# Two loads of the next batch moved ahead of the stores of the last one on SyncE's queue

## Chip, cores, metric

One core of one Trainium2 chip (trn2). The metric is the device time of one execution in microseconds (us), median over the runs. Only fast executions are compared.

## The reference, cut to what matters

Batched cross attention between x and a small state, followed by a feed-forward layer over all 4352 rows.

```python
B, H, S, Ns, D = (8, 8, 512, 32, 64)        # x: (B,H,S,D), state: (B,H,Ns,D)
scores = scale * x @ state^T                 # softmax -> xread = a  @ state
scores2 = scale * state @ x^T                # softmax -> sread = a2 @ x
t = concat([xread, sread], axis=2)           # -> rows of 512
h = t @ w_in                                 # 512 x 2048
g = h * sigmoid(1.702 * h)
out = g @ w_out                              # 2048 x 512
```

## The kernel before: the parts concerned

Batches 0 and 1 begin while the weights are still being converted to fp32. From batch 1 on, the product with w_out is done in Strassen's way (products called x, y, z below), and the attention of the next batch is cut into slots that are called after each half of a product. All loads and stores are issued on SyncE's queue, in program order (in before the last weight load at 121.77 us, the four stores from 157.78, the loads of batch 2 from 161.81).

```python
    def load_state(b):                       # 2 DMAs of 32 KB; two buffers
        stn[b] = apool.tile([P, NG, D], FP32, tag="stn", name=f"stn_{b}", bufs=2)
        for g in range(NG):
            nc.sync.dma_start(stn[b][:, g], st_v[b, g])

    def load_x(b):                           # 4 DMAs of 256 KB; one buffer (batch 1 has its own place)
        ...
        for c in range(SCH):
            nc.sync.dma_start(xn[b][:, c], x_v[b, c])

    def att_slots(b):                        # attention of batch b, slot by slot
        ...
        at(0, att_state, b)                  # transpose of the state
        for j in range(NPR):
            at(j, att_xT, b, j)              # four transposes of x each
        at(5, att_scores, b)
        ...

    def down(key, r, fs, dst, last):         # one row block f of w_out, for output rows r
        ...
        if fs[-1] == NF - 1:                 # after the last row block: store
            osb = opool.tile([P, DM], FP32, tag="osb", name=f"osb_{key}_{r}")   # two buffers
            nc.scalar.copy(osb, ops)
            nc.sync.dma_start(dst, osb)

        def product(ps, lhs, rhs, first):    # in strassen()
            for r in range(nb):              # nb = 2 halves of 16 matmuls at this size
                for f in range(HF):
                    nc.tensor.matmul(ps[:, r], lhs[f][:, P * r : P * (r + 1)], rhs[:, f], ...)
                if todo:
                    for fn, args in todo.pop(0):
                        fn(*args)

    for f in range(NF):                      # batch 0's product with w_out, 16 row blocks
        rounds(1)                            # VectorE converts weight pieces
        round_to(NFC * NPR + f + 1)
        for r in range(SCH):
            down(0, r, [f], out_x[0, r], r == SCH - 1)
        ...
        if f == NF - 2:
            T_of(T1, B12, B11)
            ...
    ...
    T_of(B12, B22, B12)
    T_of(T4, B21, T2)
    load_state(2)                            # behind the four stores of batch 0
    load_x(2)
```

Of the kernel before, what the change touches and what calls it, by code (L numbers as in the profile page):

```python
# [20 lines left out]
def kernel(  # L21
# [39 lines left out]
    NF = DF // P  # L61
# [58 lines left out]
    def load_state(b):  # L120
# [4 lines that stand above are left out]
    def load_x(b):  # L125
        if b == 1:
            xn[b] = sums[:, 0].rearrange("p (c h d) -> p c h d", c=SCH, h=H)
        else:
            xn[b] = xpool.tile([P, SCH, H, D], FP32, tag="xn", name=f"xn_{b}")
        for c in range(SCH):  # L130
            nc.sync.dma_start(xn[b][:, c], x_v[b, c])  # L131
# [89 lines left out]
    def round_to(n, ahead=AHEAD):  # L221

        while done["b"] < min(n, len(PIECES)):
            powers_to(min(done["b"] + 1 + ahead, max(NFC * NPR, done["b"] + 1)))
            round_b(done["b"])
            done["b"] += 1
            while done["b"] > NPR and done["load"] < len(PIECES) and before(done["load"]) < done["b"]:
                load_weights(done["load"] + 1)
# [114 lines left out]
    def att_M(b, c, spare=False):  # L343

        m = mpool.tile([P, NG, FC], FP32, tag="M", name=f"M_{b}_{c}")
        A[b]["M", c] = m
        name = f"M_{b}_{c}_"
        ps = [psH.tile([P, FC], FP32, tag="h", name=name + str(g)) if spare else att_ps([P, FC], name + str(g)) for g in range(NG)]
        by_state(b, ps, lambda rows, j: w_in[c][rows, j])
        for g in range(NG):  # L350
            nc.scalar.copy(m[:, g], ps[g])  # L351

    def att_eT(b, g):

        a = A[b]
        if g == 0:
            a["eT"] = apool.tile([P, NG, SCH, P], FP32, tag="eT", name=f"eT_{b}")
        ps = att_ps([P, SCH, P], f"eT_{b}_{g}")
        for c in range(SCH):
            nc.tensor.transpose(ps[:, c], a["e2"][g][0][:, P * c : P * (c + 1)], ident)  # L360
        nc.scalar.copy(a["eT"][:, g], ps)

    def att_sread(b):

        a = A[b]
        ps = att_ps([P, NG, D], f"sr_{b}")
# [3 lines that stand above are left out]
                    st = slice(Ns * j, Ns * (j + 1))  # L370
                    nc.tensor.matmul(  # L371
                        ps[st, g], a["eT"][:, g, c, st], xn[b][:, c, NG * j + g],
                        start=(c == 0), stop=(c == SCH - 1),
                    )
        sr = apool.tile([P, P], FP32, tag="sr", name=f"sr_{b}")
        nc.scalar.copy(sr, ps.rearrange("p g d -> p (g d)"))
        A[b]["sr"] = sr

    def att_srT(b):
        ps = att_ps([P, P], f"srT_{b}")  # L380
        nc.tensor.transpose(ps, A[b]["sr"], ident)
        nc.scalar.copy(srT[:, :, b, :], ps.rearrange("p (j n) -> p j n", j=NPR))
# [35 lines left out]
    def up(key, f, ntok, lhs, rhs, spare=False):  # L418
        hps = att_ps([P, ntok], f"h_{key}_{f}") if spare else psH.tile([P, ntok], FP32, tag="h", name=f"h_{key}_{f}")
        n = len(lhs)  # L420
        for i in range(n):
            nc.tensor.matmul(hps, lhs[i], rhs[i], start=(i == 0), stop=(i == n - 1))  # L422
        if f % 2 == 0:
            G[key, f // 2] = free.pop(0)
        nc.scalar.activation(out=G[key, f // 2][:, f % 2, :ntok], in_=hps, func=AF.Gelu_apprx_sigmoid)  # L425

    def up_x(b, f, spare=False):
        c, o = divmod(P * f, FC)
        m = A[b]["M", c]
        up(b, f, S, [m[:, g, o : o + P] for g in range(NG)], [A[b]["aT"][:, g] for g in range(NG)], spare)  # L430
# [10 lines left out]
    def down(key, r, fs, dst, last):  # L441

        if fs[0] == 0:
            O[key, r] = psO.tile([P, DM], FP32, tag="o", name=f"o_{key}_{r}")
        ops = O[key, r]
        for f in fs:
            nc.tensor.matmul(  # L447
                ops, G[key, f // 2][:, f % 2, P * r : P * (r + 1)], w_out[:, f], start=(f == 0), stop=(f == NF - 1)
            )
            if last and f < HF and f % 2:  # L450
                free.append(G.pop((key, f // 2)))
        if fs[-1] == NF - 1:
            osb = opool.tile([P, DM], FP32, tag="osb", name=f"osb_{key}_{r}")
            nc.scalar.copy(osb, ops)
            nc.sync.dma_start(dst, osb)
# [10 lines left out]
    def s12(key, u, ntok):  # L466

        half = ntok // 2
        (a11, a21), (_, a22) = quarters(key, u, ntok), quarters(key, HF // 2 + u, ntok)
        s1, s2 = S1[:, 2 * u : 2 * u + 2, :half], S2[:, 2 * u : 2 * u + 2, :half]  # L470
        nc.vector.tensor_tensor(out=s1, in0=a21, in1=a22, op=ALU.add)  # L471
        nc.vector.tensor_tensor(out=s2, in0=s1, in1=a11, op=ALU.subtract)
# [167 lines left out]
    def rounds(n):  # L640
        round_to(done["b"] + n)
# [75 lines left out]
    def T_of(t, x0, x1):  # L717
        nc.vector.tensor_tensor(out=t, in0=x0, in1=x1, op=ALU.subtract)
# [3 lines left out]
    for f in range(NF):  # L722
        rounds(1)
# [3 lines that stand above are left out]
        if f in (0, 2):  # L727
            for g in range(NG):
                att_eT(f // 2, g)
        if f in (0, nper * 2):  # L730
            att_M(1, 2 + f // (nper * 2))
        if f in (1, 3):
            att_sread(f // 2)
        if f in (2, 4):
            att_srT(f // 2 - 1)
        if f % 2 == 1:
            up_x(1, rest.pop(0))
        if f == NF - 2:
            T_of(T1, B12, B11)
            for u in range(NU - 1):  # L740
                s12(1, u, S)
            T_of(T2, B22, T1)
# [2 lines left out]
        s3(1, u, S)  # L745
    T_of(B12, B22, B12)
    T_of(T4, B21, T2)
    load_state(2)
    load_x(2)

    nb = P // Ns
    for b in range(1, B):
# [45 lines left out]
```

## Time and profile before

| | before |
|---|---|
| median of the first 3 runs | 764.88 us (763.66 to 765.04) |
| span of the profiled execution | 762.4 us |
| TensorE busy | 746.1 us, 98% |
| x's first half to y's first half, batch 1 (161.26 to 176.21 us) | 14.95 us |
| the same place, batch 2, less two groups of other matmuls there | 7.90 us |

TensorE is nearly always busy, so the question is where it is not, or where its clock is low. The lines are in the prediction: a stall for the loads of state and x between the halves of product x, and a clock of 0.50 from about 3 us into it. How to read them: a timeline line gives start, length, engine, source line, what, and in brackets how long the engine was idle before it and what ended that; a windows line gives each engine's busy us in a stretch, then the granted clock of TensorE (1.00 is full), the DMA engines' busy share and GB/s. "The chain" is a third view: it follows the work that ended last back from each step to what released it. It counts overlapping matmuls once, so the 16 that take 3.62 us on the timeline take 3.45 there.

### The profile page before, as it was taken

The page shows a single profiled execution, that of the slowest core. Times are in us where ns is not written, and L with a number is a line of the kernel's source. Part 1 is how long each engine was busy: PE and PEld are TensorE (multiplying, and loading weights), DVE is VectorE, ACT ScalarE, POOL GpSimd, SP SyncE. Part 2 cuts the span into 40 slices and gives each one's busy share as a digit, 9 for nine tenths or more (in the row PEclk, how much of TensorE's full clock was granted, in tenths as well). Part 3 has the DMA queues.
Part 4 walks back from the last instruction along what each step waited for, and adds up shares of the span by engine and source line. Part 5 has one row for each costly group of instructions (what it writes and reads, how often), then busy time and mean ns, then how long its engine had stood idle before and what let it go on. Part 6 is the DMA issues. An engine that isn't in the chain of part 4 may idle for free.

```text
span 762.4 us, 9847 instructions
## 1 busy us (share of the span) xinstructions
PE 746.1 (98%) x4169; PEld 565.3 (74%) x4171; DVE 414.0 (54%) x712; ACT 231.8 (30%) x411; POOL 0.8 (0%) x8
## 2 busy tenths in 40 slices
PE   8989999989999999999999999999999999999997
PEld 3433444448788878887788778887888778888886
DVE  5999799640746465463636274637355560215511
ACT  4676511021414231433134141424143312104200
POOL 0000000000000000000000000000000000000000
PEclk9999999999999999999999999999999999999999
DMA  9821242040013000300040002100030000000001
GB/s 234 324 65 52 87 157 83 0 114 1 15 42 60 1 15 28 73 1 1 28 88 0 1 28 58 30 1 15 28 73 1 15 29 15 0 21 8 0 15 41
DMA packets 48763, 35.22 MB, mean 46 GB/s; under 512 B 36432, under 2 KB 44112, under 8 KB 48720
## 3 DMA queue, kind: packets, MB, share of 16 engines
q1 hardware_dynamic: 48720, 34.61, 15.8%
q8 instruction: 32, 0.52, 0.3%
q14 instruction: 11, 0.09, 0.0%
HBM read 25.69 MB, written 8.91 MB: 45 GB/s over the span
## 4 chain that ended last, share of the span: by engine, by line
PE 94%; SPq 2%; DMA 1%; ACT 1%; issue 0%; DVE 0%; ACTq 0%
PE y L494 19%; PE z L494 13%; PE x L494 13%; PE upy L578 8%; PE h L422 7%; PE o L447 7%; PE upz L578 5%; PE upx L578 5%; PE M L276 4%; PE h_sr L422 4%; PE xT L258 2%; SPq L131 1%; PE y_sr L494 1%; PE sr L371 1%; PE s L276 1%; PE z_sr L494 1%
## 5 line engine op out<-in xcount | busy, mean ns | idle before, releaser
L494 PE MATMUL x<-w_out,g 128*128 128x256 f32 x448 | 102.4, 385 | 0.0
L494 PEld LDWEIGHTS x<-w_out,g 128*128 128x128 f32 x448 | 85.9, 194 | 12.0 <-issue 0.5
L587 DVE TENSOR_TENSOR g<-upy,g 128x512 f32<-128x512 f32 x72 | 48.1, 689 | 68.7 <-PE upy L578 68.7
L584 ACT ACTIVATE g<-g 128x512 f32<-128x512 f32 x72 | 44.8, 630 | 84.8 <-DVE g L587 84.8
L422 PE MATMUL h<-aT,M 128*128 128x512 f32 x128 | 59.6, 611 | 4.4 <-ACT M L351 4.4
L351 ACT COPY M<-M 128x512 f32<-128x512 f32 x64 | 33.2, 596 | 95.0 <-PE M L276 95.0
L422 PEld LDWEIGHTS h<-aT,M 128*128 128x128 f32 x128 | 24.1, 194 | 37.6 <-issue 24.9
L494 PE MATMUL z<-sums,later 128*128 128x256 f32 x224 | 51.1, 382 | 0.0
L494 PE MATMUL z<-w_out,g 128*128 128x256 f32 x224 | 50.8, 382 | 0.0
L494 PE MATMUL y<-sums,g 128*128 128x256 f32 x224 | 50.5, 379 | 0.0
L494 PE MATMUL y<-sums,later 128*128 128x256 f32 x224 | 50.5, 379 | 0.0
L494 PE MATMUL y<-w_out,g 128*128 128x256 f32 x224 | 50.1, 382 | 0.0
L494 PEld LDWEIGHTS z<-sums,later 128*128 128x128 f32 x224 | 42.1, 190 | 10.5 <-issue 5.0
L494 PEld LDWEIGHTS y<-w_out,g 128*128 128x128 f32 x224 | 42.1, 190 | 10.5 <-issue 5.0
L578 PE MATMUL upy<-ta,M 128*128 128x256 f32 x192 | 49.3, 379 | 0.0
L578 PE MATMUL upx<-aT,M 128*128 128x256 f32 x192 | 49.3, 379 | 0.0
L494 PEld LDWEIGHTS z<-w_out,g 128*128 128x128 f32 x224 | 41.6, 190 | 6.2
L494 PEld LDWEIGHTS y<-sums,g 128*128 128x128 f32 x224 | 41.6, 190 | 5.2
L494 PEld LDWEIGHTS y<-sums,later 128*128 128x128 f32 x224 | 41.6, 190 | 5.2
L471 DVE TENSOR_TENSOR later<-g,g 128x512 f32<-128x512 f32 (+1 forms) x32 | 20.8, 651 | 40.7 <-ACT g L425 40.7
L511 DVE TENSOR_TENSOR osb<-z,later 128x512 f32<-128x512 f32 x14 | 9.7, 692 | 60.5 <-PE z L494 60.5
L578 PEld LDWEIGHTS upx<-aT,M 128*128 128x128 f32 x192 | 36.5, 190 | 5.0
(130 smaller groups left out, 1023.6 us busy)
## 6 DMA issues: line engine op xcount, KB each, us to landing
later<-in_moe_w_out_dram SPq DMA_DIRECT2D x16, 512.0 KB
out_dram<-osb SPq DMA_DIRECT2D x32, 256.0 KB
xn<-in_x_dram SPq DMA_DIRECT2D x28, 256.0 KB
w_out<-in_moe_w_in_dram SPq DMA_DIRECT2D x12, 512.0 KB
later<-in_moe_w_in_dram SPq DMA_DIRECT2D x4, 512.0 KB
sums<-in_x_dram SPq DMA_DIRECT2D x4, 256.0 KB
stn<-in_state_dram SPq DMA_DIRECT2D x16, 32.0 KB
out_dram<-osb_sr SPq DMA_DIRECT2D x4, 128.0 KB
```

Of the source, the lines that this page charges most:

```text
L131: nc.sync.dma_start(xn[b][:, c], x_v[b, c])
L258: nc.tensor.transpose(ps[:, c], x_heads(b, c, j), ident)
L276: nc.tensor.matmul(ps[g][st], A[b]["stT"][rows, st], rhs(rows, j), start=True, stop=True)
L351: nc.scalar.copy(m[:, g], ps[g])
L422: nc.tensor.matmul(hps, lhs[i], rhs[i], start=(i == 0), stop=(i == n - 1))
L447: nc.tensor.matmul(ops, G[key, f // 2][:, f % 2, P * r : P * (r + 1)], w_out[:, f], start=(f == 0), stop=(f == NF - 1))
L471: nc.vector.tensor_tensor(out=s1, in0=a21, in1=a22, op=ALU.add)
L494: nc.tensor.matmul(ps[:, r], lhs[f][:, P * r : P * (r + 1)], rhs[:, f], start=(first and r == 0 and f == 0), stop=(f == HF - 1), skip_grou ...
L511: nc.vector.tensor_tensor(out=o, in0=ps, in1=with_, op=ALU.add)
L578: nc.tensor.matmul(ps[:, k], lhs[:, o : o + P], rhs, start=(first and k == 0), stop=True, skip_group_check=True)
L584: nc.scalar.activation(out=dst, in_=src, func=AF.Gelu_apprx_sigmoid)
L587: nc.vector.tensor_tensor(out=dst, in0=ps, in1=x, op=ALU.add)
```

## The change

The loads of batch 2 have free buffers long before they are issued (batch 0's x was last read at 94.3 to 95.4 us, the loads go out from 161.81); SyncE, in order, stands at the stores, for 35.7 us before the first. So the loads are put ahead of them.

```diff
@@ -735,6 +735,9 @@
             att_srT(f // 2 - 1)
         if f % 2 == 1:
             up_x(1, rest.pop(0))
+        if f == NF - 4:
+            load_state(2)
+            load_x(2)
         if f == NF - 2:
             T_of(T1, B12, B11)
             for u in range(NU - 1):
@@ -745,8 +748,6 @@
         s3(1, u, S)
     T_of(B12, B22, B12)
     T_of(T4, B21, T2)
-    load_state(2)
-    load_x(2)
```

## The prediction

> **What bounds the kernel now.** I read the page first: if TensorE is busy almost all the time, a change can gain only where TensorE stands still or runs slowly.
>
> ```profile
> PE 746.1 (98%) x4169; PEld 565.3 (74%) x4171; DVE 414.0 (54%) x712; ACT 231.8 (30%) x411; POOL 0.8 (0%) x8
> ```
>
> TensorE is the bound; the chain that ended last is 94% TensorE by its own line on the page. Between 200 and 760 us it is busy 558.3 of 560 us, so nothing is to be had there. What the change touches is the loads of `xn` and `stn`, so I asked for TensorE's own waits between 140 and 200 us. There are only two kinds, and both are on these loads (total us, times, longest):
>
> ```profile
> PE xT L258 <- DMA xn<-in_x_dram: 3.0, 4, 0.9
> PE stT L249 <- DMA stn<-in_state_dram: 0.5, 1, 0.5
> ```
>
> Over the whole execution the first of these groups is the same 3.0 us and 4 times: batches 3 to 7 never wait for x. So there is a single place. The timeline of TensorE there (start, length, what, idle before and its releaser):
>
> ```profile
> 161.26 3.62 PE L494 MATMUL x<-w_out,g 128*128 128x256 f32 x16
> 165.36 0.30 PE L249 MATMUL stT<-ident,stn 128*128 128x128 f32 x1 [0.48 <-DMA stn<-in_state_dram]
> 166.48 0.30 PE L258 MATMUL xT<-ident,xn 128*128 128x128 f32 x1 [0.82 <-DMA xn<-in_x_dram]
> ...
> 169.84 0.48 PE L258 MATMUL xT<-ident,xn 128*128 128x128 f32 x1 [0.54 <-DMA xn<-in_x_dram]
> 170.11 5.82 PE L494 MATMUL x<-w_out,g 128*128 128x256 f32 x16
> 175.77 0.60 PE L258 MATMUL xT<-ident,xn 128*128 128x128 f32 x4
> 176.21 3.62 PE L494 MATMUL y<-sums,later 128*128 128x256 f32 x16
> ```
>
> Batch 1's first Strassen product x is cut in two groups of 16 matmuls. Between them stand the five transposes that begin batch 2's attention (one of the state, four of x), and TensorE runs in program order, so each of the five holds the second group until its load lands. The second thing to see is the length of that second group: 5.82 us for the same 16 matmuls that took 3.62 just before. The windows say why (busy us of each engine, then granted clock, DMA share, GB/s):
>
> ```profile
> 164.00:167.00 3.00, 1.47 (x7) 0.69 (x5) 3.00 (x5) 0.27 (x1) 0.00 (x0) 1.00 1.10 223
> 167.00:168.00 1.00, 0.37 (x1) 0.14 (x1) 1.00 (x1) 0.00 (x0) 0.00 (x0) 0.87 1.35 223
> 168.00:174.00 6.00, 4.63 (x12) 3.53 (x13) 2.32 (x2) 0.59 (x1) 0.00 (x0) 0.50 0.19 33
> 174.00:175.00 1.00, 1.00 (x5) 0.86 (x4) 0.00 (x0) 0.00 (x0) 0.00 (x0) 0.71 0.09 16
> 175.00:176.00 1.00, 1.00 (x8) 0.85 (x7) 0.00 (x0) 0.00 (x0) 0.00 (x0) 1.00 0.00 0
> ```
>
> The granted clock falls to a half about 3 us into the stall, and stays there until about 174.6, some 4.5 us after the last load landed. So the stall is paid twice: as waiting, and as slow matmuls afterwards. For comparison, the same place one batch later, where the loads had long landed (its clock is 1.00 throughout):
>
> ```profile
> 248.20 3.62 PE L494 MATMUL x<-w_out,g 128*128 128x256 f32 x16
> ...
> 253.38 0.27 PE L249 MATMUL stT<-ident,stn 128*128 128x128 f32 x1
> 253.49 0.60 PE L258 MATMUL xT<-ident,xn 128*128 128x128 f32 x4
> 253.93 3.62 PE L494 MATMUL x<-w_out,g 128*128 128x256 f32 x16
> ...
> 257.82 3.62 PE L494 MATMUL y<-sums,later 128*128 128x256 f32 x16
> ```
>
> Last, why the loads come late: the timeline of SyncE's queue.
>
> ```profile
> 121.77 0.33 SPq L160 DMA_DIRECT2D later<-in_moe_w_out_dram  x1
> 157.78 3.94 SPq L455 DMA_DIRECT2D out_dram<-osb  x4
> 161.81 1.13 SPq L123 DMA_DIRECT2D stn<-in_state_dram  x2
> 163.05 2.89 SPq L131 DMA_DIRECT2D xn<-in_x_dram  x4
> ```
>
> SyncE issues the last weight load at 121.77 us and then stands for 35.7 us (the queue's longest wait for ACT's osb copies) before the first of batch 0's four stores. The loads of batch 2 are behind these stores in the program, so they begin at 161.81 although their buffers were free long before: the old x of batch 0 was last read by its sread at 94.3 to 95.4 us, the old state before that.
>
> [...] six loads with nothing of their own to wait for stood behind the stores for 40 us. [...] 1.00 to 0.50 some 3 us into the stall, 0.50 for about 6.9 us (0.13 x 2 + 6 + 0.58, from the mean clocks of the windows). [...]
>
> **The change, part by part.** It adds and removes no instruction on any engine: the instruction order shows the same rows on TensorE, VectorE, ScalarE and GpSimd, and on SyncE only the six loads moved ahead of the four stores, right after the last load of w_out. "Four row blocks sooner" is where the lines stand in the program; what counts is when SyncE gets there, and it is free at 122.10 us (121.77 + 0.33).
> - *Loads.* Issue from 122.1, 3.2 us for six (161.81 to 164.98 now), the last piece landing 4.8 us after its issue (165.03 to 169.80 in the chain). Expected landed: 122.1 + 3.2 + 4.8 = 130.1, say 132 behind the weight load. They are needed at 164.9: over 30 us to spare.
> - *Waiting removed.* In the chain the first group of x ends at 164.88 and the second starts at 170.32: 5.44 us. Five transposes without waiting cost, from batch 3, 0.11 + 0.44 = 0.55 us in the chain. Removed: 5.44 - 0.55 = 4.89 us.
> - *Slow matmuls removed.* The second group takes 5.62 us in the chain, a warm one 3.45: 2.17 us, if the clock no longer falls.
> - *Stores.* They are issued when ACT's copies are done, 157.78 and on, as now, since SyncE has been idle for some 30 us by then. No cost.
> - *Sum.* 4.89 + 2.17 = **7.06 us**. Check by the other batch: x to y is now 176.21 - 161.26 = 14.95; one batch later 257.82 - 248.20 = 9.62, less the 8 up-projection matmuls between (two groups of 0.86 in the chain) 7.90. The difference is 7.05.
>
> All of it is on the path that sets the end: from 176 us on TensorE is busy without a gap worth naming, so what starts 7 us sooner ends 7 us sooner. From the median 764.88 that gives 757.8, from the profiled execution (764.29) 757.2. I predict **757.5 us**, 1.0% less.
>
> **The rivals.**
> 1. *Another wait takes the place of the one removed.* The y product would now start at about 169.3 instead of 176.2. It needs S2 and T2. VectorE's last S2 piece ends at 163.50 (162.81 + 0.69), T2 at 148.54: 5.8 us of slack are left. VectorE goes on with s3 and two T sums until 170.31, but their first user (y's second product, with T3 finished at 168.12) starts at 193.8 now and 186.7 then. VectorE's next task after them is 13.5 us idle ahead of it, ScalarE is idle 3 to 5 us before each x copy. The new order also shows y's matmuls waiting for two DMA semaphores that were not named there before; I read them as the old weight loads into the same buffer, or at worst batch 0's first stores, landed near 160.7 to 162. Each costs nothing. If instead y waited for the last T sum, 1 us would be lost: 758.5.
> 2. *Only the waiting goes, the clock falls all the same.* Then 4.9 us: 760. Against it: with the same work and no stall the clock is 1.00 in batches 3 to 7.
> 3. *The early loads collide.* They share the DMA engines with the last weight piece, and at 122 to 136 us VectorE is over 96% busy turning such pieces into w_out. But the last piece is first touched at 132.95, while it should land near 124.5, and TensorE is then some five row blocks behind VectorE (row block 12 is being converted at 122.4 and multiplied after 144). A few us of delay would be absorbed. If it were not: up to 1 or 2 us back, 759.
> 4. *Hidden anyway, gain near zero.* The waits named above speak against it.
>
> **Range and chances.** The gain is read off one profiled execution; the three times of before spread over 1.4 us, and the moment at which the clock comes back may vary by some tenths between executions. With rival 1's 1 us on one side and spread on both, I take 756.3 to 759.2. A gain of over 2% would need 749.6, twice what the stall is worth: 1%. Slower by over 2% would need a collision of 15 us: 0.5%. Within 2%: 98.5%.
>
> **What would show each step right or wrong.** In the profile after: the six loads at about 122 to 125.5 on SyncE's queue, the stores still near 157.8; no wait of TensorE for xn or stn after 100 us; five transposes taking about 0.6 us between the groups of x; the second group of x 3.62 us long, the clock 1.00 from 164 to 176; y starting near 169.2; everything from there to the end shifted by 7 us with equal durations. The prediction is wrong if y shows a wait of its own, if the clock still falls, if TensorE begins to wait for w_out between 122 and 160 us, or if a later batch waits for x or a store.

The sum is 4.89 + 2.17 = 7.06 us, both terms read from the trace. The 124.5 us of rival 3 is an estimate from the profile before, in which the DMA share is 0.65 from 124 to 124.5 us and 0.02 in the half microsecond after.

## The result, and the profile after

| | before | after |
|---|---|---|
| median | 764.65 us (763.66 to 765.04, 4 runs) | 757.47 us (757.20 to 757.98, 4 runs) |
| ratio of the fast runs | | 0.9909, 95% interval 0.9892 to 0.9926 |
| span of the profiled execution | 762.4 us | 755.7 us |
| mean granted clock | 0.993 | 0.998 |
| x's first half to y's first half | 14.95 us | 7.89 us |

A ratio is the mean time of one kernel's fast runs over that of the other's of the same rounds, so it is not quite the ratio of the medians. The interval lies clear of 1.

TensorE's timeline of the changed kernel at the same place:

```profile
161.62 3.62 PE L494 MATMUL x<-w_out,g 128*128 128x256 f32 x16
165.08 0.27 PE L249 MATMUL stT<-ident,stn 128*128 128x128 f32 x1
165.19 0.60 PE L258 MATMUL xT<-ident,xn 128*128 128x128 f32 x4
165.62 3.62 PE L494 MATMUL x<-w_out,g 128*128 128x256 f32 x16
...
169.51 3.62 PE L494 MATMUL y<-sums,later 128*128 128x256 f32 x16
```

No line has an idle time in brackets any more, and the second half of x takes 3.62 us where it took 5.82. The windows of the same kernel show the clock that goes with it:

```profile
167.00:168.00 1.00, 1.00 (x7) 0.87 (x5) 1.00 (x1) 0.00 (x0) 0.00 (x0) 1.00 0.00 0
168.00:174.00 6.00, 6.00 (x33) 5.31 (x32) 2.68 (x2) 1.47 (x3) 0.00 (x0) 1.00 0.01 3
```

And SyncE's queue of the changed kernel:

```profile
122.51 1.14 SPq L123 DMA_DIRECT2D stn<-in_state_dram  x2
123.69 3.67 SPq L131 DMA_DIRECT2D xn<-in_x_dram  x4
158.14 3.95 SPq L455 DMA_DIRECT2D out_dram<-osb  x4
```

The loads go out from 122.5 to 127.4 us and the DMA engines are idle again by about 130 (share 1.10 from 125 to 130 us, 0.03 from 130 to 135). The stores come out when ACT's copies are done, as before.

Where the 6.7 us of span went: the stage x to y is 7.06 us shorter (14.95 - 7.89), and the changed kernel's execution came to this stage 0.36 us later (161.62 against 161.26). Of that, 0.31 us is a group of 16 h matmuls at 42 us that took 8.83 us instead of 8.52, far ahead of the change; the experiment warm_start deals with that place.

### The profile page after: what moved, and what is told of

It is laid out like the page before. It is cut to its first block, busy times and chain, and to the rows that moved or that the text cites. A ratio compares the mean times of both kernels' runs of the same rounds, so it can differ in the third digit from the quotient of the medians.

```text
span 755.7 us, 9853 instructions
## 1 busy us (share of the span) xinstructions
PE 743.6 (98%) x4171; PEld 563.8 (75%) x4171; DVE 413.9 (55%) x712; ACT 231.7 (31%) x411; POOL 0.8 (0%) x8
## 4 chain that ended last, share of the span: by engine, by line
PE 96%; SPq 2%; ACT 1%; DMA 1%; issue 0%; DVE 0%; ACTq 0%
PE y L494 19%; PE z L494 13%; PE x L494 13%; PE upy L578 8%; PE h L422 8%; PE o L447 7%; PE upx L578 5%; PE upz L578 5%; PE M L276 4%; PE h_sr L422 4%; PE xT L258 2%; PE y_sr L494 1%; SPq L131 1%; PE sr L371 1%; PE s L276 1%; PE z_sr L494 1%
## 5 line engine op out<-in xcount | busy, mean ns | idle before, releaser
L494 PE MATMUL x<-w_out,g 128*128 128x256 f32 x448 | 100.2, 379 | 0.0
L494 PEld LDWEIGHTS x<-w_out,g 128*128 128x128 f32 x448 | 84.2, 190 | 11.4 <-ACT osb L454 0.2
```

## The experiments

Theory: the loads sat behind the stores for no reason of their own; TensorE paid for it twice, by 4.89 us of waiting and by 2.17 us of slow matmuls because its clock had fallen during the wait. (Of the 4.89 us, 3.52 are the idle times in brackets in the prediction's lines and others of the same kind; the other 1.37 are the five transposes, which take 1.92 us one by one and 0.55 in a row.) Rivals: the row block at which the loads stand matters; the DMA traffic itself costs something; the clock falls for another reason; the price is simply in proportion to the wait. Every kernel gave correct results. The runs below the first two rows of this table were done on three chips, each with its own runs of the kernel before (medians 764.53, 764.40 and 764.95 us). "x to y" is read from each kernel's own timeline, as above.

| run | x to y, us | median, us | ratio to before, 95% interval |
|---|---|---|---|
| (before) | 14.95 | 764.65 | |
| (after) | 7.89 | 757.47 | 0.9909 (0.9892 to 0.9926) |
| just_ahead | none: slow execution | 756.90 (the four fast) | 0.9905 (0.9890 to 0.9920) |
| just_ahead_2 | 7.89 | 756.90 | 0.9900 (0.9883 to 0.9917) |
| early_f3 | 7.90 | 757.63 | 0.9911 (0.9895 to 0.9927) |
| x_only | 8.55 | 757.95 | 0.9912 (0.9898 to 0.9927) |
| state_only | 13.34 | 761.97 | 0.9973 (0.9959 to 0.9988) |
| after_two | 9.83 | 759.29 | 0.9930 (0.9917 to 0.9943) |
| awake | 12.72 | 761.99 | 0.9974 (0.9957 to 0.9990) |
| slots_later | (other order) | 757.28 | 0.9906 (0.9891 to 0.9921) |
| warm_start | 7.90 | 755.85 | 0.9890 (0.9878 to 0.9903) |
| warm_before | 14.85 | 763.26 | 0.9978 (0.9964 to 0.9993) |

### Does the row block matter? just_ahead and early_f3

```diff
 # just_ahead: after row block 14, straight before the block that stores
-        if f == NF - 4:
+        if f == NF - 2:
             load_state(2)
             load_x(2)
 # early_f3: among the weight loads
-        if f == NF - 4:
+        if f == 3:
             load_state(2)
             load_x(2)
```

> The six loads stand after row block 14, just ahead of the four stores, instead of after row block 12. Theory (what counts is only to be ahead of the stores, since SyncE is free from 122 us): the queue issues them at the same 122 to 126 us, and the time is that of the changed kernel, 757.5 us (757.0 to 758.0). Rival (the row block at which they stand decides when they are issued): issue near 153 us; the time would still be about 757.5, but the queue's timeline would show it.

The first run's profile fell on an execution of 1313.42 us with a mean clock of 0.557, so nothing in it can be compared by time. Its other four took 755.83 to 757.86 us. The mean clock of that execution was 0.82 over the first 10 us, 0.55 from 10 to 100 us and 0.56 from 300 to 400 and from 1000 to 1300 us; nothing in these runs explains it. I repeated it:

> The kernel of just_ahead once more, unchanged: the profile of its first run fell on an execution at a clock of 0.56 throughout (1313 us), which cannot be laid beside the others. Expected in a fast execution: SyncE issues the six loads at 122 to 126 us, straight behind the last weight load, and the time is 757.5 us, or 755.9 us in executions whose clock shows 1.000.

The queue issued the state at 123.41 us, straight behind the last weight load (87.79 + 35.56 = 123.35), though the lines now stand behind row block 14. So "four row blocks sooner" is not what the change does: it takes the loads from behind the stores, which is 39 us sooner (161.81 - 122.51). The rival is out for places behind the last weight load. Ahead of it the place does move the issue, as the next run shows, but not the time.

> The six loads stand after row block 3, in the middle of the weight loads of w_out (ahead of the last six), where VectorE is busy without a gap and each weight load is issued only when a buffer comes free. Theory (each piece has about three pieces of VectorE's work, some 10 us, between its issue and its use, and the six loads take 3.2 us to issue and 5 us to move): no delay, 757.5 us. Rival (the early loads collide with the weight pieces): VectorE waits for pieces of w_out, TensorE for VectorE, and 1 to 5 us are lost, 758.5 to 762 us.

Here the queue of early_f3 shows the loads in the middle of the weights:

```profile
86.94 14.43 SPq L160 DMA_DIRECT2D later<-in_moe_w_out_dram  x5
101.42 1.14 SPq L123 DMA_DIRECT2D stn<-in_state_dram  x2
102.60 4.25 SPq L131 DMA_DIRECT2D xn<-in_x_dram  x4
106.95 15.57 SPq L160 DMA_DIRECT2D later<-in_moe_w_out_dram  x6
```

Even so VectorE waits for nothing between 95 and 136 us, and the time is that of the changed kernel (757.63 us against 757.47). No collision shows, even among the weight loads.

### Which load? x_only and state_only

```diff
 # x_only (state_only: the two calls exchanged)
+        if f == NF - 4:
+            load_x(2)
 ...
     load_state(2)
-    load_x(2)
```

> Only the four loads of x stand ahead of the stores, the two of the state behind them. The state lands near 165.4 us as before (SyncE reaches it at 161.8), x long before. Theory: TensorE waits about 0.5 us for the state, then runs on; no fall of the clock; 757.5 + 0.5 = 758.0 us. Rival (the first wait matters as much as the others): 760 us or more.

As the theory said: one wait of 0.47 us for the state remains, no fall of the clock, 757.95 us.

> Only the two loads of the state stand ahead of the stores, the four of x behind them. SyncE reaches the loads of x 1.2 us sooner (161.8 instead of 163.0), so the last lands near 168.6. Theory: the stall is some 3.8 us in place of 5.4, long enough that the clock most likely still falls, later and for less of the group's work; time 757.5 + 3.3 to 5.5, most likely 762.5 us. Rival (the state's load is what starts the stall, so that alone brings most of the gain): 759 us or less.

Also as expected: 761.97 us, 0.53 under the value called most likely. The line of x's second half and the windows around it in state_only:

```profile
167.63 5.30 PE L494 MATMUL x<-w_out,g 128*128 128x256 f32 x16
```

```profile
167.00:168.00 1.00, 0.53 (x2) 0.48 (x3) 1.00 (x1) 0.15 (x1) 0.00 (x0) 0.82 0.00 0
168.00:174.00 6.00, 6.00 (x24) 5.01 (x23) 0.93 (x1) 1.02 (x3) 0.00 (x0) 0.75 0.01 3
```

The clock fell just as the last load landed, and matmuls with nothing to wait for ran slowly: 5.30 us for the 16. It fell for about 0.36 + 3.0 = 3.4 us (0.18 x 2 in the first window, half of 6 us in the second). The six executions spread widely, 761.00 to 763.94 us, with clocks from 0.997 down to 0.993. The profile shows only one of the faster ones, 761.14 us. In it the clock did not fall at this kernel's other stall, at 40 us (see warm_start; the h matmuls behind it took 7.13 us), where it fell in the profiled executions of before, after and awake (8.52, 8.83 and 8.83 us).

### Is the clock's part in proportion to the wait? after_two

```diff
 # from the kernel before, its own loads removed
         for r in range(SCH):
             down(0, r, [f], out_x[0, r], r == SCH - 1)
+            if f == NF - 1 and r == 1:
+                load_state(2)
+                load_x(2)
```

> The six loads stand behind the first two stores and ahead of the last two. They can then be issued from about 159.1 us and the last x lands near 159.1 + 3.2 + 4.8 = 167.1 us, 2.7 us sooner than before. Theory (the stall is paid twice[...]): stall of about 2.3 us in place of 5.4, granted clock stays at 1.00, second group of x at 3.45 us; time 757.5 + 1.7 = 759.2 us. Rival (waiting and slow matmuls shrink in proportion, or any stall costs the clock): 757.5 + 7.1 x 0.38 = 760.2, or with the whole 2.2 us of slow matmuls 761.4 us.

In the stall of 2.12 us at 40 us the clock of before fell.

TensorE's timeline of after_two:

```profile
165.08 0.38 PE L258 MATMUL xT<-ident,xn 128*128 128x128 f32 x2
166.28 0.33 PE L258 MATMUL xT<-ident,xn 128*128 128x128 f32 x1 [0.81 <-DMA xn<-in_x_dram]
167.29 0.33 PE L258 MATMUL xT<-ident,xn 128*128 128x128 f32 x1 [0.69 <-DMA xn<-in_x_dram]
167.46 3.62 PE L494 MATMUL x<-w_out,g 128*128 128x256 f32 x16
```

The waits add up to 1.5 us, the clock is 1.00 in every window from 164 to 176 us, and the second half of x is at full speed. The stage is 1.94 us longer than after (9.83 - 7.89), the time 1.8 us (759.29 - 757.47; expected 1.7). So here the second price was a step, not a share: part of the wait came back, and nothing of the slow matmuls. By the times (759.3 to 759.6 us in three executions, 757.7 and 757.9 in two) none of the five seems to have paid it, though only the first was profiled. What the traces show of where the step lies is under "Why the prediction was right".

### The clock's part alone: awake

The kernel before, with small bf16 matmuls (results unused) in the stall.

```diff
+    def awake(n):
+        ps = psH.tile([P, FC], FP32, tag="h", name="awake")
+        m = ident.bitcast(mybir.dt.bfloat16)
+        for _ in range(n):
+            nc.tensor.matmul(ps[:, : 2 * P], m[:, :P], m, start=True, stop=True)
 ...
+        if b == 2:
+            at(0, awake, 26)
         at(0, att_state, b)
```

> The kernel before, with 26 small bf16 matmuls on the identity (results unused) put ahead of the five transposes of batch 2, in the time in which TensorE waits. The loads come as late as before. Theory (of the 7.06 us, 2.2 us are slow matmuls that follow from the idle time itself): the second group of x still starts near 170.1 us, the clock stays at 1.00, the group takes 3.45 us instead of 5.62, and the time falls by 2.2 to 2.4 us to 762.3 us. Rival (the clock falls for another reason, the DMA traffic or the batch's beginning): the group stays at 5.6 us and the time at 764.6 us or a little more.

TensorE's timeline of awake:

```profile
162.31 3.62 PE L502 MATMUL x<-w_out,g 128*128 128x256 f32 x16
165.76 3.00 PE L388 MATMUL awake<-ident 128*128 128x256 bf16 x26
...
171.14 3.62 PE L502 MATMUL x<-w_out,g 128*128 128x256 f32 x16
```

From the first to the second half of x it is 8.83 us, as before (170.11 - 161.26 = 8.85): the waiting is all still there. The second half takes 3.62 us instead of 5.82, x to y is 2.23 us shorter (14.95 - 12.72), the clock 1.00. The median is 2.5 us under that of the kernel before in the same rounds (764.53 - 761.99), by the ratio 2.0 us. One of the six executions, 764.49 us at a clock of 0.995, was as slow as before; its trace was not kept, so why stays open. This separates the two terms: the loads and their traffic are as late as before, so it is the idle time that brings the slow matmuls, and work that computes nothing saves them.

### Leave the loads, move the reader: slots_later

```diff
-        at(0, att_state, b)
+        late = b == 2
+        at(2 if late else 0, att_state, b)
         for j in range(NPR):
-            at(j, att_xT, b, j)
+            at((2, 3, 3, 4)[j] if late else j, att_xT, b, j)
```

> The kernel before with its late loads, but the transposes of batch 2 are put two slots later: state and first x block after the first half of y, near 171.8 us, two more after the second half of y, the last after the first half of the next x. The last load lands at 169.8. Theory (the cost is TensorE's wait at that place alone): no wait, clock at 1.00, the same 757.5 us (757.0 to 758.3) with the loads where they were. Rival (earlier loads also help by taking DMA traffic out of this stage, or y waits for VectorE's sums once it starts at 168.3): 758.5 us or more.

The loads are as late as ever (SyncE issues them from 162.06 to 166.29 us), but TensorE's timeline has the transposes where they have landed:

```profile
161.51 7.07 PE L495 MATMUL x<-w_out,g 128*128 128x256 f32 x32
168.42 3.62 PE L495 MATMUL y<-sums,later 128*128 128x256 f32 x16
171.87 0.27 PE L249 MATMUL stT<-ident,stn 128*128 128x128 f32 x1
```

757.28 us: the whole gain without moving a load. So it is the wait at this one place, and neither the DMA traffic under product x (share 1.32 from 166 to 168 us; the 32 matmuls took 7.07 us) nor VectorE's sums (y starts at 168.4 here, sooner still than after the change) showed a cost.

### Another stall of the same kind: warm_start and warm_before

At 40 to 42 us TensorE waits 2.1 us for ScalarE's copies of M (the product of state and w_in, from which h is formed); the next 16 matmuls of h are slow, 8.83 us for the 16, where the 16 at 31 us took 7.13. In the changed kernel:

```profile
38.14 1.84 PE L276 MATMUL M<-w_in,stT 64*32 64x512 f32 x16
42.10 8.83 PE L422 MATMUL h<-aT,M 128*128 128x512 f32 x16 [2.12 <-ACT M L351]
50.86 1.09 PE L276 MATMUL M<-w_in,stT 64*32 64x512 f32 x16
```

```diff
     att_M(1, 0)
+    keep_warm(10)          # the kernel's own dummy bf16 matmuls
```

> The changed kernel, with ten dummy matmuls more in another stall of the same kind: at 39.2 to 42.1 us TensorE waits for ScalarE's copies of M, and the next 16 matmuls of h take 8.83 us instead of 7.1 at a clock of 0.50. Theory of the double price: the 1.7 us of slow matmuls there vanish. But in this stage VectorE is over 96% busy on w_in, and the next M at 50.9 waits for its last piece of w_in done at 50.6: so I expect that the gain is given back there, 757.3 us (at most 0.3 us). Rival (it lies on the path that sets the end): 755.8 us.

Here my expectation was wrong and the rival right: 755.85 us, the fastest of all: 1.6 us under the changed kernel (757.47 - 755.85; by the ratios, 0.9890 against 0.9911 for early_f3, 1.6 us too). In warm_start:

```profile
40.24 2.33 PE L115 MATMUL warm<-sums 128*128 128x512 bf16 x10
42.43 7.13 PE L422 MATMUL h<-aT,M 128*128 128x512 f32 x16
49.49 1.09 PE L276 MATMUL M<-w_in,stT 64*32 64x512 f32 x16
```

I had read that the next M at 50.86 us waits for VectorE's piece of w_in that ends at 50.61. It does not: here M starts at 49.49, while VectorE's piece runs until 50.60. Two ends that lay 0.25 us apart were a coincidence, not a release.

> The kernel before with the ten dummy matmuls of warm_start at its early stall. Theory (the early stall cools the clock in most executions but not in all, which is where the spread of 1.5 us comes from; the stall at 165 us is a second, separate loss): all executions at a clock of 0.995 and 763.2 us, spread under 0.6 us; the difference to warm_start (755.85) is again 7.1 to 7.4 us. Rival (the two stalls share their cost): 761.5 us or below, or the spread stays at 1.5 us.

All six executions have clocks of 0.995 to 0.997, median 763.26 us, 7.41 us above warm_start on another chip. So the two stalls cost separately. The spread did not shrink as I expected (762.53 to 763.76 us, not under 0.6). Its profiled execution reaches its first M matmuls at 30.18 us where the first profile of before did at 29.17, ahead of either stall, so part of it comes from the start of the program. I did not follow that further.

The clocks of single executions also tell where the two levels of many runs come from. In the three sets of eleven runs of before, those at a clock of 0.993 took 764.4 to 766.5 us, those at 0.995 763.0 to 763.6, and the three at 0.994 lie at 763.8 to 764.3. In just_ahead, just_ahead_2, slots_later, x_only and early_f3 those at 0.997 or 0.998 took 757.3 to 758.7 us, those at 1.000 755.8 to 756.5. (Level by level the change is worth the same: on the lower-clock level the means of before and of these runs without x_only are 765.05 and 757.81 us, on the other 763.32 and 756.09, 7.2 us apart both times.) That fits the early stall cooling the clock in most executions and not in all; state_only's profile shows one where it did not (h in 7.13 us after the same 2.12 us of waiting).

## Why the prediction was right

- **Loads.** Expected to be issued from 122.1 us and landed by 130 to 132; 122.5 and about 130. just_ahead_2 shows that the place behind the last weight load has no part in it.
- **Waiting removed, 4.89 us.** The stage in the chain is free of waits. awake keeps the waiting and loses only the rest; after_two and x_only leave parts of it in place, 1.94 and 0.66 us of stage.
- **Slow matmuls removed, 2.17 us.** The second half of x went from 5.82 to 3.62 us. awake shows this term alone, 2.23 us of stage. Rival 2 (the clock falls all the same) is refuted.
- **Sum, 7.06 us.** The stage got shorter by 7.06 us, the medians differ by 7.18. That 757.47 us lies within 0.03 of the 757.5 predicted is luck, though, for the prediction did not foresee that executions come on two levels. All four here were at a clock of 0.997 or 0.998. Of the 18 fast executions of just_ahead, just_ahead_2, slots_later and early_f3, seven were at 1.000, and six of these, 755.8 to 756.2 us, lie under the predicted range.
- **Rival 1** (y waits for VectorE or for the two newly named semaphores): y shows no wait after the change, nor in slots_later where it starts earlier still. That the semaphores stand for old weight loads was my reading, and no run needed it.
- **Rival 3** (collision with weight loads): none, not even in early_f3. Why there was no delay, no run here shows.
- **Smaller numbers of the prediction that are off**, without harm: the clock came back 4.8 us after the last load landed (174.57 - 169.80), not 4.5; the half clock's three parts add up to 6.84 us, not 6.9; the six issues took 4.9 us (122.51 to 127.36), not 3.2; a result 2% slower than before would have needed a loss of some 22 us (15.3, and the 7.1 gained), not 15; and the lines moved ahead by three row blocks in the program, from behind block 15 to behind block 12.

What the traces show of the clock's fall. Read in steps of 0.05 us, the half clock lasted 3.41 us at 41 us in before (41.45 to 44.86) and at 43 us in after (42.96 to 46.37), and 6.83 us in product x of before (167.74 to 174.57); from coarser windows it is about 3.4 us in product x of state_only and 6.8 us in that of warm_before. The prediction's "some 3 us into the stall" is not a fixed delay. From the end of x's first half to the fall it was 2.9 us in before (164.88 to 167.74) and about 4.15 us in state_only (163.49 to 167.64); from the start of the stall at 40 us it was 1.5 us in before (39.92 to 41.45) and 3.0 us in after (39.98 to 42.96), where TensorE was at work again when it came. These are the stalls of the traces in the stretches that were read, by the waits in brackets on TensorE's timeline:

| execution | stall | waits in it, us | clock in or after it | matmuls behind it, us |
|---|---|---|---|---|
| before | in x | 3.52 (five) | 0.50 | 5.82 |
| warm_before | in x | 3.46 (five) | 0.51 (mean, 168 to 174 us) | 5.68 |
| state_only | in x | 2.91 (four) | 0.50 | 5.30 |
| before | at 40 us | 2.12 | 0.50 | 8.52 |
| after | at 40 us | 2.12 | 0.50 | 8.83 |
| awake | at 41 us | 2.12 | 0.50 | 8.83 |
| state_only | at 40 us | 2.12 | 1.00 | 7.13 |
| awake | in x, behind the dummies | 1.56 (two) | 1.00 | 3.62 |
| after_two | in x | 1.50 (two) | 1.00 | 3.62 |
| before, after, state_only, warm_start | at 50 to 53 us | 1.50 | 1.00 | 5.42 (12 of h) |
| x_only | in x | 0.47 | 1.00 | 3.62 |

So in these stretches the clock fell wherever TensorE waited for 2.91 us or more, and nowhere with 1.56 us or less; at 2.12 us it fell in three executions and not in a fourth. What decides there was not shown. All this was read from the traces afterwards; no run was made to test it.

One thing the prediction missed without being hurt by it: it took the 1.4 us of spread for noise. Much of it is the early stall's clock, which warm_start removes (its four executions, all at a clock of 1.000, took 755.64 to 756.18 us).

## What to carry to other kernels

On an in-order queue, ask of every load whether what stands ahead of it waits for something that the load itself does not need (here six loads stood behind four stores for 40 us); where a line stands in the program says little about when it is issued (just_ahead_2 has the lines two row blocks later than the changed kernel, and its loads still go out straight behind the last weight load). Price a TensorE stall twice: its idle time, and the matmuls after it at half clock (here 4.89 and 2.17 us). The second price was a step here: in the stretches read it was paid after waits of 2.91 us or more and not after 1.56 us or less, and the same stall of 2.12 us paid it in before and after and escaped it in state_only. Dummy matmuls inside a stall that stays saved it in awake (26 of them, 2.0 to 2.5 us) and in warm_start (ten, 1.6 us).
